# An attention and mixture-of-experts kernel: the last group's places scattered before the first expert's tokens are scaled, tokens transposed tile by tile, the first expert in two halves of 240 columns

## The chip, the cores and the metric

The kernel runs on one core of one Trainium2 chip. The metric is device time in microseconds (us), the median of several executions. A profile of one execution stands beside it; the prediction's sums are made against that execution.

## What is computed

Three stages are chained over 2304 tokens of 512 numbers (4 sequences of 576, 8 heads of 64).

```
scores = scale * q @ k.T                       # window of 32 keys: plain for heads 0-3, every 4th key for heads 4-7
x = softmax(where(mask, scores, -1e9)) @ v     # -> [2304, 512]

logits = x @ w_gate                            # 8 experts
e_idx = argmax(logits); gate_w = softmax(logits)[e_idx]; eom = sigmoid(x @ w_output_gate)
for e in range(8):                             # only tokens with e_idx == e
    out[mask] = gate_w * eom[:, e] * (relu(x[mask] @ w1[e]) @ w2[e])      # 512 -> 1024 -> 512

h = relu(out @ w_in); result = (h * h) @ w_out                            # 512 -> 2048 -> 512
```

## The kernel before

**Attention and routing.** Tokens come in 18 tiles of 128, in six groups (`GROUPS`: tiles 0-2, 3-6, 7-10, 11-12, 13-14, 15-17). For each tile TensorE multiplies q by k, VectorE and ScalarE make the softmax, TensorE multiplies by v, and the token rows x go to the table `x_d` in HBM (`store`, L495). For each group `lg` makes the gate's logits and `route1` to `route6` choose each token's expert and its place in that expert's list. `route5` (L580) ends with a cast of the places into the tile `di` (L599). `scatter` (L611, issue at L615) then has GpSimd write, by indirect DMA, one row per token into `meta_d`, the lists of all experts; a group of n columns takes n scatters. `di` comes from the pool `wk`, which has two buffers for each name, so a group's `di` has the buffer of the group two before it, and the cast waits until that group's scatters have landed.

**The first expert.** After group 4 (tokens 0 to 1919, `EARLY` = 15 tiles) `choose` picks the expert with most tokens so far. Its first weights are loaded (`load_w`, L114: pieces of 128 x 1024 numbers, 512 KB, eight to an expert, into three staging buffers `raw`), and the front of its list is read (`meta_load`, L133), its token rows gathered (`gather`, L138) and scaled (`scale`, L149) by the gate's weight while group 5 is still being routed. So the first expert is worked in two halves, `WD` entries 0 and 1, of `HALF` columns each: the first half holds only places that the first 1920 tokens have filled. `conv_w` (L119) splits a weight piece for the matmuls: ScalarE casts it to a reduced-precision float (L123), VectorE subtracts to get the rest (L124). `xsplit` (L154) does the same for tokens, ScalarE at L157 and VectorE at L158. Every product is three matmuls: high x high, high x low, low x high (`mm3`, L784).

**The order around the change** is written out by hand at the end of `attention` (L716 to L734): after the last tile come the logits of group 5, `warm(6)` (matmuls of ones that nobody reads), the conversion of weight piece 0, `route1` to `route4` of group 5, two more `warm` matmuls, the loads of pieces 2 and 3, the stores of the last tiles, then `scale(0)`, `transposes(0)` (L161), `conv_w(0, 1)`, `route5(5)`, and `scatter(5)`. `transposes(0)` takes both tiles of 128 tokens in turn, with the four blocks of 128 features of a tile going to four PSUM tiles in four banks; after the second tile it calls `xsplit` on each of the four.

**The experts** (`experts`, L736). GpSimd's queue starts with `meta_load(1)` and `gather(1)`, the second half of the first expert (L971, L972); the list of the second half needs the scatters of group 5. Then for each of the nine windows of `WD` come eight steps of `up` (L789: 12 matmuls, then ScalarE's relu L799 and VectorE's rest L800) and four of `down` (L805: 24 matmuls). In window 0, the first half, pieces 2 to 7 of the expert's weights are converted after steps 1, 3, 5, 6, 7 and 8. `scale(1)` stands after the second `down`, and `transposes(1)` after the third, so that the fourth `down` is behind them on TensorE. A window of n columns is 192 matmuls of n columns. The windows (`WIN`) are 512 (two halves of 256), 384, 336, 320, 304, 288, 256 and 256 columns for the experts in order of their size.

**The last stage** works on 2304 columns in six blocks of 384, and ends with indirect DMAs of the rows to their places.

Of the kernel before, what the change touches and what calls it, by code (L numbers as in the profile page):

```python
# [10 lines left out]
F32 = mybir.dt.float32  # L11
F32R = mybir.dt.float32r
BF16 = mybir.dt.bfloat16
I32 = mybir.dt.int32
# [9 lines left out]
P = 128  # L24
# [8 lines left out]
EARLY = GROUPS[NG - 1][0]  # L33
E = 8
# [1 line left out]
FF = 1024  # L36
FF2 = 2048

WIN = [512, 384, 336, 320, 304, 288, 256, 256]
HALF = WIN[0] // 2  # L40
MS = NT + 256
YC = sum(WIN) + 128
NEG = -8.0e9
# [9 lines left out]
def attention_experts_kernel(ctx: ExitStack, tc: tile.TileContext, qB, kB, vB, wg, wE, wF, consts, rows, ids, out):  # L53
    nc = tc.nc
# [11 lines left out]
    ident = cpool.tile([P, P], F32, name="ident")  # L66
# [35 lines left out]
    io32 = rowc[:, 4 * E + E * E:4 * E + E * E + NSPILL]  # L102


    WD = [(0, 0, HALF), (0, HALF, HALF)] + [(r, 0, WIN[r]) for r in range(1, E)]
    NW = len(WD)
    reg = {}

# [10 lines left out]
    def conv_w(r, c):  # L119
        s = free.pop(0)  # L120
        w_t[r, c] = s
        raw, (hi, lo) = raw_t.pop((r, c)), (slots[s][:, 0], slots[s][:, 1])
        nc.scalar.copy(out=hi, in_=raw)  # L123
        nc.vector.tensor_tensor(out=lo, in0=raw, in1=hi.bitcast(F32), op=ALU.subtract)  # L124


    xg_t, xh_t, xl_t = {}, {}, {}

    def tiles(w):
        n = WD[w][2]  # L130
        return [(i, min(P, n - P * i)) for i in range((n + P - 1) // P)]

    def meta_load(w, engine=None, n="p"):  # L133
        r, s0, _ = WD[w]
        k = len(tiles(w))
        (engine or nc.gpsimd).dma_start(out=mt[:, w, 0:k], in_=meta_d[ds(reg[n, r] * MS + s0, P * k), :].rearrange("(i p) c -> p i c", p=P))
# [9 lines left out]
            )  # L146
            xg_t[w, i] = t

    def scale(w):  # L149
        for i, n in tiles(w):  # L150
            t = xg_t[w, i]
            nc.vector.tensor_scalar(out=t[:n], in0=t[:n], scalar1=mt[:n, w, i, 1:2].bitcast(F32), scalar2=None, op0=ALU.mult)

    def xsplit(src, n):  # L154
        h = stg.tile([P, TB], F32R, tag="xh", name="xh", bufs=4)
        l = stg.tile([P, TB], F32R, tag="xl", name="xl", bufs=4)
        nc.scalar.copy(out=h[:, :n], in_=src)  # L157
        nc.vector.tensor_tensor(out=l[:, :n], in0=src, in1=h[:, :n].bitcast(F32), op=ALU.subtract)  # L158
        return h, l

    def transposes(w, bank, ks=range(4)):  # L161
        n = WD[w][2]
        p = {}
        for k, (i, m) in [(k, t) for k in ks for t in tiles(w)] if w else [(k, t) for t in tiles(w) for k in ks]:
            if i == 0:
                p[k] = bank(k)
            nc.tensor.transpose(p[k][:, P * i:P * i + m], xg_t[w, i][:m, P * k:P * k + P], ident[:m, :m])
            if w and i == len(tiles(w)) - 1:
                xh_t[w, k], xl_t[w, k] = xsplit(p[k][:, :n], n)
        if not w:  # L170
            for k in ks:
                xh_t[w, k], xl_t[w, k] = xsplit(p[k][:, :n], n)


    def row_pool(tp):
# [19 lines left out]
    def order_steps(tp):  # L195
# [4 lines left out]
        def row(shape, name, dt=F32):  # L200
            return tp.tile([1] + shape, dt, name=name)
# [40 lines left out]
        yield v.reduce_sum(out=low, in_=f16, axis=AX.X)  # L242
        yield v.tensor_scalar(out=low, in0=low, scalar1=float(HALF), scalar2=None, op0=ALU.is_lt)
        big = row([1], "big1")
        yield v.tensor_scalar(out=big, in0=of[:, E - 1:E], scalar1=float(NT - WIN[-1]), scalar2=low, op0=ALU.is_lt, op1=ALU.max)
        yield v.tensor_tensor(out=sr[:, 0, :], in0=win, in1=nw, op=ALU.subtract)
# [64 lines left out]
    def attention():  # L311
        st = ExitStack()
        c2 = st.enter_context(tc.tile_pool(name="c2", bufs=1))
        wk = st.enter_context(tc.tile_pool(name="wk", bufs=2))
        ps_s = st.enter_context(tc.tile_pool(name="ps_s", bufs=2, space=PSUM))
        ps_1 = st.enter_context(tc.tile_pool(name="ps_1", bufs=1, space=PSUM))
# [7 lines left out]
        def warm(n):  # L324

            ps = ps_1.tile([P, 4, P], F32, tag="xt", name="warm")
            for _ in range(n):
                nc.tensor.matmul(out=ps, lhsT=ones, rhs=ones.unsqueeze(1).to_broadcast([P, 4, P]), start=True, stop=True)
# [36 lines left out]
        o = 2 * P  # L365
# [129 lines left out]
        def store(i, m, engine=nc.sync):  # L495
            a = i % 2
            x = x_t["pair", i // 2]
            d = x_d[P * i:P * i + m * P]
            engine.dma_start(out=d[:, 0:256].rearrange("(n p) c -> p n c", n=m), in_=x[:, a:a + m, 0:256])
            for n in range(m):  # L500
                engine.dma_start(out=d[P * n:P * n + P, 256:512].rearrange("(j r) c -> r j c", r=4), in_=x[:, a + n, 256:512])
# [25 lines left out]
        def t3(g, name, dt=F32):  # L527
            return wk.tile([P, 4, E], dt, tag=name, name=name)[:, 0:COLS[g]]

        def t2(g, name, dt=F32):  # L530
            return wk.tile([P, 4], dt, tag=name, name=name)[:, 0:COLS[g]]
# [4 lines left out]
        def rows_of(g):  # L536
            return slice(0, 96 if len(GROUPS[g]) == 3 else P)
# [42 lines left out]
        def route5(g):  # L580

            ls, e, oh = rt[g]
            rk = rk_t.pop(g)
            n, c = rows_of(g), COLS[g]
            m = idsb[:, g, 0:c]
            v = nc.vector
            zp, z, ez, se, dn = t3(g, "zp"), t2(g, "z"), t2(g, "ez"), t2(g, "se"), t2(g, "dn")
            r1, s2, di = t3(g, "r1"), t2(g, "s2"), t2(g, "di", I32)
            v.tensor_tensor(out=zp[n], in0=oh[n], in1=ls[n, :, E:2 * E], op=ALU.mult)
            v.reduce_sum(out=se[n], in_=e[n], axis=AX.X)  # L590
            v.reduce_sum(out=z[n], in_=zp[n], axis=AX.X)
            nc.scalar.activation(out=ez[n], in_=z[n], func=ACTF.Exp, scale=-1.0)
            v.tensor_tensor(out=r1[n], in0=rk[n, 0:c], in1=eoff[n, 0:c], op=ALU.add)
            v.tensor_scalar(out=se[n], in0=se[n], scalar1=1e-9, scalar2=None, op0=ALU.add)
            v.tensor_tensor(out=r1[n], in0=r1[n], in1=oh[n], op=ALU.mult)
            v.scalar_tensor_tensor(out=dn[n], in0=ez[n], scalar=1.0, in1=se[n], op0=ALU.add, op1=ALU.mult)
            v.reduce_sum(out=s2[n], in_=r1[n], axis=AX.X)
            v.reciprocal(out=m[n, :, 1:2].bitcast(F32), in_=dn[n].unsqueeze(2))
            v.tensor_copy(di[n], s2[n])  # L599
            rt[g] = di, m, oh  # L600
# [10 lines left out]
        def scatter(g, cols=None):  # L611
            di, m, _ = rt[g]
            n = rows_of(g)
            for b in cols or range(COLS[g]):
                ins = nc.gpsimd.indirect_dma_start(  # L615
                    out=meta_d, out_offset=bass.IndirectOffsetOnAxis(ap=di[n, b:b + 1].bitcast(U32), axis=0),
                    in_=m[n, b, :], in_offset=None, bounds_check=E * MS - 1, oob_is_err=False,
                ).ins
                for o in scat:
                    tc.declare_no_dep(ins, o, reason="each slot of a list is written once")  # L620
                scat.append(ins)
# [14 lines left out]
        for i in range(EARLY):  # L636
# [3 lines left out]
            t = (i + 2) % LAP  # L640
            n = i + 2 - t + LAP
# [21 lines left out]
            g = ends.get(i - 1)  # L663
# [16 lines left out]
        i, g = EARLY, NG - 2  # L680
# [44 lines left out]
        load_w(0, 3)  # L725
        store(i + 1, 1)
        store(i + 2, 1)
        scale(0)
        transposes(0, lambda k: ps_1.tile([P, 1024 if k == 2 else 512], F32, tag=("pt", "lg", "o", "xt")[k], name="xT"))
        conv_w(0, 1)  # L730
        route5(g + 1)
        scatter(g + 1)
        nc.vector.tensor_copy(cs[:, 1, :], cnt[0:1, :])
        return st  # L734

    def experts():  # L736
# [22 lines left out]
        def placed():  # L759
            v = loaded(of_t, ACTE, sum(WIN) - WIN[-1], "sums of at most the windows' lengths")  # L760
            oa.update(enumerate(v))
# [27 lines left out]
        def up(w, f):  # L789
            r, _, n = WD[w]  # L790
            s = slots[w_t[r, f // 2]]
# [13 lines left out]
        def down(w, c):  # L805
            r, _, n = WD[w]
            s = w_t[r, 4 + c]
# [6 lines left out]
            nc.scalar.copy(out=y[:, :n], in_=p[:, :n])  # L814
            at = slice(HALF * w, HALF * w + n) if w < 2 else ds(oa[r], n)
            nc.scalar.dma_start(out=yT_d[P * c:P * c + P, at], in_=y[:, :n])
# [3 lines left out]
        def ids_out(w):  # L820
            r, s0, n = WD[w]
            at = slice(HALF * w, HALF * w + n) if w < 2 else ds(oa[r], n)
            nc.scalar.dma_start(out=idc_d[at, :], in_=meta_d[ds(reg["a", r] * MS + s0, n), :])
# [326 lines left out]
def _consts():  # L1150
# [20 lines left out]
    lt = (e[None, :] < e[:, None]).astype(f)  # L1171
    rows = np.concatenate([e, E - 1 - e, np.array(WIN, f), e * MS, lt.reshape(-1), np.arange(NSPILL, dtype=f)])[None]
    return dict(consts=consts, rows=np.ascontiguousarray(rows), ids=np.ascontiguousarray(ids.reshape(P, -1)))
# [14 lines left out]
```

## Time and profile before

| what | us |
|---|---|
| median of 3 runs | 793.91 |
| lowest, highest | 791.36, 796.9 |
| the profiled execution, its own time | 794.1 |
| its span, first to last instruction | 792.4 |
| TensorE busy in the span | 736.1 (93%) |
| VectorE, ScalarE, GpSimd busy | 437.1, 328.7, 94.6 |

PE is TensorE's matmuls, PEld its weight loads, DVE VectorE, ACT ScalarE, POOL GpSimd, SP the engine that issues most DMAs. A row of a timeline gives start, duration, engine, line, operation, the tiles (written, then read), the number of instructions merged in the row, and in square brackets the time for which the engine had stood idle and what ended that. A matmul's duration is longer than the step to the next one, since matmuls overlap; a rate is read from the starts.

### The profile page before, as it was taken

The numbers are of one execution on the slowest core, as the hardware profiler recorded it, in microseconds if no ns is written. First come the engines' busy times: TensorE is split into PE (matmuls) and PEld (weight loads), VectorE is DVE, ScalarE is ACT, GpSimd is POOL, SyncE is SP. The second block draws the span as 40 slices with busy tenths as digits, with TensorE's granted clock in tenths as the row PEclk, the third lists the DMA queues.
The fourth block names the chain that finished last, engine by engine and source line by source line (L and its number), as shares of the span: only waits on it lengthen the run. The fifth ranks groups of instructions, "written<-read, shape, count | busy, mean of one in ns | idle before, by whom it ended". The sixth has DMA issues, their size and how long they took to land. (4 is left out here: it accounts for less than half of the span.)

```text
span 792.4 us, 13859 instructions
## 1 busy us (share of the span) xinstructions
PE 736.1 (93%) x5363; PEld 670.6 (85%) x5363; DVE 437.1 (55%) x888; ACT 328.7 (41%) x647; POOL 94.6 (12%) x104
## 2 busy tenths in 40 slices
PE   8767759899999999999999999999999999999993
PEld 5555539899999999999999989999889888889992
DVE  7656636477566566777677787762333333332421
ACT  3433324364454555655555555552222222222320
POOL 5234414320110110000000000000100000010101
PEclk9999869899999999999999999999999999999997
DMA  8999457474666667765444334330302012030201
GB/s 275 296 274 255 119 171 191 137 244 142 223 185 200 201 200 218 213 216 166 129 159 134 124 116 160 107 119 1 97 23 91 29 45 76 10 111 1 81 1 43
DMA packets 55073, 110.54 MB, mean 140 GB/s; under 512 B 9497, under 2 KB 30874, under 8 KB 55002
## 3 DMA queue, kind: packets, MB, share of 16 engines
q1 hardware_dynamic: 45338, 93.35, 39.0%
q0 software_dynamic: 4192, 10.77, 3.8%
q10 hardware_dynamic: 5472, 5.48, 2.0%
q8 instruction: 44, 0.72, 0.4%
q14 instruction: 27, 0.22, 0.1%
HBM read 89.62 MB, written 20.00 MB: 138 GB/s over the span
## 5 line engine op out<-in xcount | busy, mean ns | idle before, releaser
L785 PE MATMUL hp<-xh,slot 128*128 128x384 f32 (+5 forms) x672 | 216.4, 322 | 1.2 <-DVE hl L800 1.2
L787 PE MATMUL hp<-xh,slot 128*128 128x384 f32 (+5 forms) x672 | 216.1, 322 | 0.0
L786 PE MATMUL hp<-xl,slot 128*128 128x384 f32 (+5 forms) x672 | 215.7, 321 | 0.0
L785 PEld LDWEIGHTS hp<-xh,slot 128*128 128x128 f32 x672 | 127.7, 190 | 4.8 <-DVE hl L800 1.4
L786 PEld LDWEIGHTS hp<-xl,slot 128*128 128x128 f32 x672 | 127.7, 190 | 3.2 <-DVE xl L158 0.2
L787 PEld LDWEIGHTS hp<-xh,slot 128*128 128x128 f32 x672 | 127.6, 190 | 0.0
L872 DVE SCALAR_TENSOR_TENSOR g<-hp,r 128x384 f32<-128x384 f32 x96 | 53.2, 554 | 120.3 <-ACT r L871 119.8
L899 PE MATMUL op<-slot,gh 128*128 128x512 f32 x288 | 112.5, 390 | 1.9 <-ACT gh L874 1.9
L901 PE MATMUL op<-slot,gl 128*128 128x512 f32 x288 | 113.9, 395 | 0.0
L900 PE MATMUL op<-slot,gh 128*128 128x512 f32 x288 | 113.3, 393 | 0.0
L124 DVE TENSOR_TENSOR slot<-raw,slot 128x1024 fp32r<-128x1024 f32 x64 | 77.8, 1224 | 52.3 <-ACT slot L123 52.2
L871 ACT ACTIVATE r<-hp 128x384 f32<-128x384 f32 x96 | 46.9, 489 | 142.1 <-PE hp L787 141.7
L786 PE MATMUL yp<-hl,slot 128*128 128x256 f32 (+5 forms) x288 | 87.0, 302 | 1.3 <-DVE hl L800 1.2
L785 PE MATMUL yp<-hh,slot 128*128 128x256 f32 (+5 forms) x288 | 88.1, 306 | 0.1
L787 PE MATMUL yp<-hh,slot 128*128 128x256 f32 (+5 forms) x288 | 86.6, 301 | 0.0
L876 DVE TENSOR_TENSOR gl<-g,gh 128x384 fp32r<-128x384 f32 x96 | 53.5, 557 | 44.0 <-ACT gh L874 43.4
L874 ACT CAST gh<-g 128x384 fp32r<-128x384 f32 x96 | 49.2, 513 | 62.9 <-DVE g L872 62.5
L913 POOL DMA_INDIRECT out<-os,idc x18 | 17.6, 976 | 469.3 <-DVE os L912 467.8
L123 ACT CAST slot<-raw 128x1024 fp32r<-128x1024 f32 x64 | 66.4, 1051 | 14.0 <-DMA raw<-in_wE 9.4
L901 PEld LDWEIGHTS op<-slot,gl 128*128 128x128 f32 x288 | 54.0, 188 | 12.5 <-DVE gl L876 1.2
L899 PEld LDWEIGHTS op<-slot,gh 128*128 128x128 f32 x288 | 54.1, 188 | 12.3 <-ACT gh L874 3.2
L900 PEld LDWEIGHTS op<-slot,gh 128*128 128x128 f32 x288 | 54.0, 188 | 9.7
(152 smaller groups left out, 879.8 us busy)
## 6 DMA issues: line engine op xcount, KB each, us to landing
raw<-in_wE SPq DMA_DIRECT2D x63, 512.0 KB, 4.0
raw<-in_wF SPq DMA_DIRECT2D x32, 512.0 KB, 3.7
yr<-yT_d SPq DMA_DIRECT2D x48, 192.0 KB, 3.3
vb<-in_vB SPq DMA_DIRECT2D x16, 520.0 KB, 8.4
part_d<-os SPq DMA_DIRECT2D x18, 256.0 KB, 2.0
raw<-part_d SPq DMA_DIRECT2D x18, 256.0 KB, 4.3
q<-in_qB SPq DMA_DIRECT2D x8, 512.0 KB
x_d<-x SPq DMA_DIRECT2D x22, 128.0 KB
```

The lines of the kernel that those rows point to most:

```text
L123: nc.scalar.copy(out=hi, in_=raw)
L124: nc.vector.tensor_tensor(out=lo, in0=raw, in1=hi.bitcast(F32), op=ALU.subtract)
L785: nc.tensor.matmul(out=out, lhsT=wh, rhs=mh, start=first, stop=False)
L786: nc.tensor.matmul(out=out, lhsT=wh, rhs=ml, start=False, stop=False)
L787: nc.tensor.matmul(out=out, lhsT=wl, rhs=mh, start=False, stop=last)
L871: nc.scalar.activation(out=r, in_=p[:, :TB], func=ACTF.Relu)
L872: nc.vector.scalar_tensor_tensor(out=q, in0=p[:, :TB], scalar=0.0, in1=r, op0=ALU.max, op1=ALU.mult)
L874: nc.scalar.copy(out=h, in_=q)
L876: nc.vector.tensor_tensor(out=l, in0=q, in1=h.bitcast(F32), op=ALU.subtract)
L899: nc.tensor.matmul(out=o_t[j], lhsT=h[:, a], rhs=w[:, 0], start=first, stop=False)
L900: nc.tensor.matmul(out=o_t[j], lhsT=h[:, a], rhs=w[:, 1], start=False, stop=False)
L901: nc.tensor.matmul(out=o_t[j], lhsT=l[:, a], rhs=w[:, 0], start=False, stop=last)
```

## The change

Five edits. The window of the first expert is 480 columns instead of 512, and `HALF` is 240 (15 x 128 / 8), so 32 fewer columns are worked. `di` gets a tag of its own with four buffers. `conv_w(0, 1)`, `route5`, `scatter` of group 5 and the copy of the counts now stand ahead of the scaling of the first half's tokens. Three more `warm` matmuls follow them. The first half's tokens are then scaled and transposed tile by tile, with five `warm` matmuls between the two tiles; the four feature blocks go to two PSUM banks of the pool `ps_s`, two blocks of 256 columns in each, instead of to four banks. (`scale` can now take one tile alone, and `transposes` has lost its branch for window 0; for the other windows both do what they did.)

```
-WIN = [512, 384, 336, 320, 304, 288, 256, 256]
-HALF = WIN[0] // 2
+WIN = [480, 384, 336, 320, 304, 288, 256, 256]
+HALF = EARLY * P // E
...
-            r1, s2, di = t3(g, "r1"), t2(g, "s2"), t2(g, "di", I32)
+            r1, s2, di = t3(g, "r1"), t2(g, "s2"), wk.tile([P, 4], I32, tag="di", name="di", bufs=4)[:, 0:c]
...
         store(i + 2, 1)
-        scale(0)
-        transposes(0, lambda k: ps_1.tile([P, 1024 if k == 2 else 512], F32, tag=("pt", "lg", "o", "xt")[k], name="xT"))
         conv_w(0, 1)
+
         route5(g + 1)
         scatter(g + 1)
         nc.vector.tensor_copy(cs[:, 1, :], cnt[0:1, :])
+        warm(3)
+        banks = [ps_s.tile([P, 512], F32, tag="s", name="xT") for _ in range(2)]
+        for t in tiles(0):
+            scale(0, t)
+            j, n = t
+            for k in range(4):
+                nc.tensor.transpose(banks[k // 2][:, 256 * (k % 2) + P * j:256 * (k % 2) + P * j + n], xg_t[0, j][:n, P * k:P * k + P], ident[:n, :n])
+            if j == 0:
+                warm(5)
+        n = WD[0][2]
+        for k in range(4):
+            xh_t[0, k], xl_t[0, k] = xsplit(banks[k // 2][:, 256 * (k % 2):256 * (k % 2) + n], n)
```

On VectorE, at the end of the routing of group 5 and the start of window 0, these instructions stood in a row before (`xg` are gathered tokens, `xl` the low part of the transposed ones, `slot` a converted weight piece, `di` the places):

```order
L565 TENSOR_TENSOR oh<-eq,m_1779 96x32
L152 TENSOR_SCALAR xg<-xg,mt 128x512 x2
L158 TENSOR_TENSOR xl<-xT,xh 128x256 x4
L124 TENSOR_TENSOR slot_91<-raw,slot_91 128x1024
L589 TENSOR_TENSOR zp<-oh,ls 96x32
L590 TENSOR_REDUCE se<-ex 96x4
L591 TENSOR_REDUCE z<-zp 96x4
```

and now, at the end of `route5` of group 5, which has its line 592 to 595 here, this stands in a row:

```order
L592 SCALAR_TENSOR_TENSOR dn<-ez,se 96x4
L593 TENSOR_REDUCE s_1810<-r_1809 96x4
L594 RECIPROCAL idsb<-dn 96x4
L595 CAST di<-s_1810 96x4
L728 COPY cs<-rk 1x8
L153 TENSOR_SCALAR xg<-xg,mt 128x512
L153 TENSOR_SCALAR xg<-xg,mt 112x512
L159 TENSOR_TENSOR xl<-xT,xh 128x240 x4
L807 SCALAR_TENSOR_TENSOR hl<-hp,hh 128x240 x2
```

The weight piece, the ten instructions of `route5` and the copy of the counts have moved from behind the tokens' scaling and splitting to ahead of them.

On ScalarE, at the same place, before (with what each instruction waits for; `xh` is the high part of the transposed tokens):

```order
L552 ACTIVATE ex<-d 96x32 [waits DVE_49]
L157 CAST xh<-xT 128x256 [waits PE_49] x4
L123 CAST slot_91<-raw 128x1024 [waits DMAHW7_49]
L592 ACTIVATE ez<-z 96x4 [waits DVE_49]
L799 ACTIVATE hh<-hp 128x256 [waits DMAHW4_49,DMAHW6_49,DMAHW1_49,PE_49]
```

and now:

```order
L548 ACTIVATE ex<-d 96x32 [waits DVE_49]
L124 CAST slot_91<-raw 128x1024 [waits DMAHW7_49]
L588 ACTIVATE ez<-z 96x4 [waits DVE_49]
L158 CAST xh<-xT 128x240 [waits PE_49]
L158 CAST xh<-xT 128x240 [waits DVE_49]
L158 CAST xh<-xT 128x240 [waits PE_49]
L158 CAST xh<-xT 128x240 [waits DVE_49]
L806 ACTIVATE hh<-hp 128x240 [waits DMAHW4_49,DMAHW6_49,DMAHW1_49,PE_49]
```

The second and the fourth cast, which share a bank with the one ahead of them, now wait for VectorE, which reads that bank too.

## Rows read from the trace of the kernel before

**Rows 1.** Windows by stage: length; busy us of PE, PEld, DVE, ACT, POOL; clock; DMA.
```profile
115.00:148.41 33.41, 29.23 (x202) 28.46 (x202) 19.58 (x55) 13.28 (x26) 16.49 (x18) 0.82 0.60 160
148.41:171.46 23.05, 23.05 (x196) 23.05 (x195) 17.07 (x36) 13.47 (x26) 3.64 (x3) 1.00 0.52 161
171.46:782.20 610.74, 603.71 (x3437) 560.49 (x3435) 332.86 (x582) 263.07 (x504) 30.42 (x31) 1.00 0.38 121
```

**Rows 2.** Windows cut where TensorE's granted clock changes; columns as in rows 1.
```profile
106.43:120.08 13.65, 8.27 (x37) 6.57 (x37) 5.31 (x21) 2.67 (x7) 2.38 (x3) 0.50 0.55 164
120.08:140.56 20.48, 18.18 (x149) 17.67 (x147) 12.59 (x28) 9.54 (x16) 10.00 (x12) 1.00 0.76 204
140.56:147.39 6.83, 4.95 (x24) 4.87 (x24) 2.91 (x10) 1.49 (x4) 4.74 (x6) 0.50 0.40 112
```

**Rows 3.** Timeline, DVE: the end of route5 of group 4.
```profile
92.57 0.17 DVE L598 RECIPROCAL idsb<-dn 128x2 f32<-128x2 f32 x1
94.25 0.17 DVE L599 CAST di<-s 128x2 int32<-128x2 f32 x1 [1.51 <-DMA meta_d<-idsb,di]
```

**Rows 4.** Timeline: from the scatters of group 4 to the first half's tokens.
```profile
94.70 0.99 POOL L615 DMA_INDIRECT meta_d<-idsb,di  x1 [2.45 <-DVE rs L479]
...
105.13 1.05 POOL L142 DMA_INDIRECT xg<-x_d,mt  x1 [8.16 <-DMA x_d<-x]
...
110.06 0.49 DVE L152 TENSOR_SCALAR xg<-xg,mt 128x512 f32<-128x512 f32 x1 [3.35 <-DMA xg<-x_d,mt]
...
113.53 0.48 DVE L152 TENSOR_SCALAR xg<-xg,mt 128x512 f32<-128x512 f32 x1 [2.98 <-DMA xg<-x_d,mt]
```

**Rows 5.** Timeline: the first half's second tile, its split, and matmuls of window 0.
```profile
114.07 1.11 PE L167 MATMUL xT<-ident,xg 128*128 128x128 f32 x4 [2.35 <-DVE xg L152]
114.58 1.20 ACT L157 CAST xh<-xT 128x256 fp32r<-128x256 f32 x4 [8.42 <-PE xT L167]
114.98 1.42 DVE L158 TENSOR_TENSOR xl<-xT,xh 128x256 fp32r<-128x256 f32 x4 [0.97 <-ACT xh L157]
...
116.05 0.41 PE L785 MATMUL hp<-xh,slot 128*128 128x256 f32 x1
...
119.68 0.41 PE L787 MATMUL hp<-xh,slot 128*128 128x256 f32 x1
```

**Rows 6.** Timeline: from the scatters of group 5 to the second half's tokens on TensorE.
```profile
119.32 1.01 POOL L615 DMA_INDIRECT meta_d<-idsb,di  x1 [11.21 <-DVE cs L733]
...
129.38 0.76 POOL L136 DMA_DIRECT2D mt<-meta_d  x1 [5.36 <-DMA meta_d<-idsb,di]
...
134.03 1.07 POOL L142 DMA_INDIRECT xg<-x_d,mt  x1 [3.90 <-DMA mt<-meta_d]
...
140.31 0.33 PE L167 MATMUL xp<-ident,xg 128*128 128x128 f32 x1 [2.13 <-DVE xg L152]
...
141.98 0.49 DVE L152 TENSOR_SCALAR xg<-xg,mt 128x512 f32<-128x512 f32 x1 [1.72 <-DMA xg<-x_d,mt]
...
142.52 1.75 PE L167 MATMUL xp<-ident,xg 128*128 128x128 f32 x7 [1.88 <-DVE xg L152]
143.93 0.56 PE L785 MATMUL yp<-hh,slot 128*128 128x256 f32 x1
```

**Rows 7.** Timeline, PE: starts of matmuls of 256 and of 384 columns at full clock.
```profile
148.41 0.28 PE L785 MATMUL hp<-xh,slot 128*128 128x256 f32 x1
...
151.17 0.28 PE L787 MATMUL hp<-xh,slot 128*128 128x256 f32 x1
...
179.51 0.33 PE L785 MATMUL hp<-xh,slot 128*128 128x384 f32 x1
...
182.45 0.33 PE L787 MATMUL hp<-xh,slot 128*128 128x384 f32 x1
```

**Rows 8.** Timeline, ACT: weight pieces 5 and 6 of window 0 being cast.
```profile
128.93 1.05 ACT L123 CAST slot<-raw 128x1024 fp32r<-128x1024 f32 x1 [0.82 <-DMA raw<-in_wE]
...
131.88 1.05 ACT L123 CAST slot<-raw 128x1024 fp32r<-128x1024 f32 x1 [1.62 <-DMA raw<-in_wE]
```

More of the change, by code (lines that the diff above doesn't have):

```diff
@@ L102, in attention_experts_kernel @@
     io32 = rowc[:, 4 * E + E * E:4 * E + E * E + NSPILL]
-    WD = [(0, 0, HALF), (0, HALF, HALF)] + [(r, 0, WIN[r]) for r in range(1, E)]
+    WD = [(0, 0, HALF), (0, HALF, WIN[0] - HALF)] + [(r, 0, WIN[r]) for r in range(1, E)]
     NW = len(WD)
@@ L147, in gather, with scale @@
             xg_t[w, i] = t
-    def scale(w):
-        for i, n in tiles(w):
+    def scale(w, only=None):
+        for i, n in tiles(w) if only is None else [only]:
             t = xg_t[w, i]
@@ L162, in transposes @@
         n = WD[w][2]
[L163 to L172, printed above, removed]
+        for k in ks:
+            p = bank(k)
+            for i, m in tiles(w):
+                nc.tensor.transpose(p[:, P * i:P * i + m], xg_t[w, i][:m, P * k:P * k + P], ident[:m, :m])
+            xh_t[w, k], xl_t[w, k] = xsplit(p[:, :n], n)
     def row_pool(tp):
```

## The prediction

> **What bounds the kernel now.** First the busy time of each engine by stage. From 171.46 us on TensorE is busy for 603.71 of 610.74 us, and from 148.41 to 171.46, in the second half of the first expert, for all of it, at full clock [rows 1]. There only fewer or shorter matmuls would help. From 115.00 to 148.41, in the first half of the same expert, it is busy for 29.23 of 33.41 us at a mean clock of 0.82 [rows 1]. The work is the same 192 matmuls and takes 10.36 us longer (33.41 - 23.05). So the stretch before 148.41 is the place to look at.
>
> Then the clock. TensorE was granted 0.50 (1.2 GHz) from 106.43 to 120.08 and again from 140.56 to 147.39, and 1.00 (2.4 GHz) between and after [rows 2]. In the first of the two it worked for 8.27 of 13.65 us, waits for tokens between [rows 2]; the second came right after it had stood idle for 2.13 us [rows 6].
>
> Then, by the timeline, what it waited for. The first expert needs tokens that are scaled at 110.06 and 113.53, after waits of 3.35 and 2.98 us for the gather; the gather itself was issued at 105.13, at the end of a chain that starts with the scatters of group 4 at 94.70 [rows 4]. The second half needs the scatters of group 5. GpSimd had stood idle for 11.21 us when it could issue the first of them at 119.32, because `route5` stood behind the first half's tokens on VectorE. From there the chain runs on: read of the list 129.38, gather 134.03, last tokens scaled 141.98 [rows 6], 22.7 us in all (141.98 - 119.32). TensorE waits for it, 2.13 and 1.88 us [rows 6].
>
> **The change part by part.**
>
> A. The places' own buffers. The cast of group 4's places waited 1.51 us for the scatters of group 2 [rows 3], and the scatter, `choose`, the list and the gather of rows 4 all hang on it. With four buffers group 4 has group 0's, whose scatters are long done. What is late next is data that is there: the products of the tile that follows it. I let the whole 1.5 us come through to the first tokens (bounds: 0, if the gather is held by other transfers, to 1.5).
>
> B. The clock at the start. Between 116.05 and 119.68 lie 17 matmul steps, 0.2135 us each; at full clock 23 steps take 2.76 us, 0.120 each [rows 5, 7]. So a step at half clock costs 0.0935 more. Some 20 matmuls from 115.00 to 120.08 run so: 1.9 us, and the four transposes of the second tile, 1.11 us merged [rows 5], lose another 0.4. The change lays five filler matmuls into the wait of 2.35 us before the second tile, and three before the first. If TensorE then has its full clock when the split is done, 2.3 us go. The fillers themselves run where it would wait. I take 2.0 (bounds 0 and 2.3).
>
> C. The split costs more. Before, four casts on ScalarE took 1.20 us and four subtractions on VectorE 1.42, shifted by 0.40 (114.58 and 114.98): 1.82 in all [rows 5]. Two blocks now share a bank, and the order has the second and fourth cast wait for VectorE. Then a cast (0.30), a subtraction (0.36), and so on alternate, with an overlap only where the bank changes: about 2.6 us. The first `up` also writes a bank that the split still reads. Loss 0.8 (bounds 0 and 1.5).
> The Trainium skill has a rule for this (PSUM — Partial Sum Buffer, Terms): no two of the three engines may access one bank in the same cycle, reads against reads included. In rows 5 the blocks had a bank each and the engines did overlap, which agrees; by the rule C is the 0.8 that I take, without it C would be 0 and the time 0.8 lower.
>
> D. The second half's list. `route5` and the weight piece ahead of the scaling fill the 3.35 us for which VectorE waited for the gather anyway [rows 4], so they delay nothing. The places are then ready near 108 instead of 119, and the scatters go out some 11 us earlier. With the same 22.7 us the second half's tokens are scaled near 131, and TensorE, which came to that place at 138.18 (140.31 - 2.13), comes to it near 135 after A to C and half of E, and need not wait. What goes: from the first transpose's wait to the next `down` it took 2.13 + (143.93 - 140.31) = 5.75 us, and eight transposes without a wait need about 1.0 at full clock (seven took 1.75 at half [rows 6]), so 4.75. Then sixteen matmuls between 143.93 and 147.39 at half clock, 16 x 0.0935 = 1.5 us. Together 6.2 (bounds 2 and 6.2). The second half's list read and gather stay on the same queue, and nothing else is moved past them.
>
> E. Fewer columns. Two windows of 192 matmuls lose 16 columns each. Steps of 0.120 us for 256 columns and 0.173 for 384 (17 steps from 179.51 to 182.45) [rows 7] give 0.42 ns per column, so 6.7 ns a matmul, and 384 x 6.7 ns = 2.6 us. But no matmul of this kind in the profile has fewer than 256 columns. Bounds: from 2.6 gained to what the third rival says. I take the straight line, which the rows keep between 256 and 384.
>
> F. What gets late next in window 0. The weights come through three buffers: pieces 5 and 6 were cast at 128.93 and 131.88 after waits of 0.82 and 1.62 us for their transfers [rows 8], each of which starts when an earlier piece is converted. Piece 4 now starts some 9 us earlier, since piece 1 is converted earlier; the others follow TensorE's own steps and shift with it, but TensorE's steps get shorter than the transfers. Also the scaling of the second half's tokens stands behind piece 7 on VectorE. I put 1.0 us on this (bounds 0 and 3).
>
> Sum: 1.5 + 2.0 - 0.8 + 6.2 + 2.6 - 1.0 = 10.5 us. The profiled execution took 794.1 us, span 792.4 and 1.7 around it, and stands 0.2 above the median of 793.91, so no correction is made: 794.1 - 10.5 = 783.6 us. That is 1.3% less. A measurement of this kernel tells about 1% from no change, 7.9 us.
>
> **The rivals.**
>
> 1. The narrow matmul takes as long as one of 256 columns. For it: none shorter is to be seen, and at each step a weight load of 128 columns goes by; against it: the line from 384 to 256 shows no bend [rows 7]. Then E is gone: 786.2.
>
> 2. The second half's tokens stay late, or a weight piece does. The chain of rows 6 is mostly transfer time, 5.36 and 3.90 us in two waits; now it runs beside the stores of the last tiles and two weight loads. If TensorE still waits 2 us and its clock drops once more, D shrinks to 2.5: 787.3. Against it: some 4 us of slack by D.
>
> 3. Slower: the matmul of 240 columns is slower than that of 256. Place: all 384 matmuls of windows 0 and 1. For the price the trace has a second kind of row: plain fp32 transposes of 128 columns, seven in 1.75 us at half clock [rows 6], step by step as long as a matmul of 256 columns there (0.21), so two cycles a column. If a matmul below 256 columns fell to that rate it would cost like 480 columns, 0.214 us: 384 x 0.094 = 36 us more, against gains of 7.9 in A to D and F: 822. It decides from 0.141 us a matmul (7.9 / 384 = 0.021 above 0.120). For it only that every window is 256 or more; against it that the type and the three products stay the same.
>
> 4. The clock stays low to 120 in spite of the fillers; B gives 0: 785.6. For it: after 115.00 the engine worked without a gap and still had its full clock only from 120.08 [rows 2]; against it: the fillers start the work some 3 us sooner.
>
> 5. What moves was hidden after all, by transfers that hold both gathers: about 791.
>
> **How the numbers follow.** Forecast 0.38, rival 1 0.20, rival 2 0.12, rival 3 0.15, rival 4 0.10, rival 5 0.05. Faster by over 1% means under 786.0: nearly all of the forecast (0.36), half of rivals 1 and 4 (0.15), a little of 2 (0.01): 0.52. Slower by over 1% is rival 3: 0.15. The rest, 0.33, lies within 1%. The range goes from all gains at their upper bounds with C and F at 0 (12.6, which is 781.5, and 1.5 for the spread of the runs) to rival 5: 780.0 to 791.0. It leaves out rival 3 and a few hundredths. The forecast's own range is 781.5 to 786.
>
> **What would show it.** The cast of group 4's places without a wait, and the first half's last tokens scaled near 112. Scatters of group 5 before 110. A granted clock of 1.00 at the first `up` and no drop until the end. No wait of TensorE for scaled tokens before the fourth `down` of window 0, which then ends near 139. Steps of 0.113 us in windows 0 and 1. I am wrong if the step is 0.120 or more (E), if TensorE waits for `xg` again (D), if weight casts wait longer than 2 us for their transfers (F), or if the clock is 0.50 after 115 (B).

## The result and the profile after

The changed kernel takes 784.93 us, the median of 6 runs (782.14 to 789.08); the kernel before, beside it, 792.95 us (791.36 to 796.9). The ratio is 0.9899, with a 95% interval from 0.9866 to 0.9932: 8.0 us, or 1.0%, less. The forecast was 783.6. The profiled execution took 785.35 us, with a span of 783.6, 8.8 less than the span before.

First the windows, which answer to [rows 1] and [rows 2]: busy time by stage, then cut where the granted clock changes (columns as there).
```profile
117.41:141.99 24.58, 24.25 (x201) 24.06 (x201) 15.19 (x39) 11.38 (x22) 11.55 (x14) 0.94 0.58 180
141.99:165.01 23.02, 23.02 (x206) 22.89 (x205) 17.31 (x40) 14.16 (x26) 4.79 (x4) 1.00 0.62 184
165.01:783.60 618.59, 602.37 (x3426) 559.30 (x3424) 332.70 (x582) 262.13 (x503) 30.51 (x30) 0.99 0.37 119
...
99.95:110.19 10.24, 6.50 (x81) 3.81 (x81) 4.61 (x13) 4.07 (x10) 2.69 (x3) 1.00 0.85 190
110.19:120.43 10.24, 7.23 (x28) 5.30 (x28) 3.82 (x18) 1.60 (x6) 4.08 (x5) 0.50 0.55 194
120.43:141.99 21.56, 21.24 (x189) 21.04 (x188) 14.52 (x37) 10.96 (x21) 11.46 (x14) 1.00 0.66 203
```
The first half of the first expert went from 33.41 to 24.58 us: TensorE now works through it with 0.33 us of idle time, and the second stretch at a clock of 0.50 [rows 2] is gone. But it starts 2.4 us later (117.41 against 115.00), and the first stretch at 0.50 still reaches into it, to 120.43. The second half went from 24.33 (148.41 to 172.74, the same 192 matmuls with the transposes between them) to 23.02, and what follows took 618.59 us against 619.66 (172.74 to the end).

Then the timeline after, whose rows answer to [rows 3] to [rows 7].
```profile
95.79 0.17 DVE L594 RECIPROCAL idsb<-dn 128x2 f32<-128x2 f32 x1
95.99 0.17 DVE L595 CAST di<-s 128x2 int32<-128x2 f32 x1
96.44 0.98 POOL L611 DMA_INDIRECT meta_d<-idsb,di  x1 [1.33 <-DVE rs L475]
...
111.54 0.47 DVE L153 TENSOR_SCALAR xg<-xg,mt 128x512 f32<-128x512 f32 x1
111.83 1.05 POOL L611 DMA_INDIRECT meta_d<-idsb,di  x1 [2.87 <-DVE cs L728]
...
113.00 0.49 DVE L153 TENSOR_SCALAR xg<-xg,mt 112x512 f32<-112x512 f32 x1 [0.99 <-DMA xg<-x_d,mt]
...
115.73 0.36 ACT L158 CAST xh<-xT 128x240 fp32r<-128x240 f32 x1 [4.78 <-issue]
116.12 0.41 DVE L159 TENSOR_TENSOR xl<-xT,xh 128x240 fp32r<-128x240 f32 x1 [2.63 <-ACT xh L158]
116.56 0.62 ACT L158 CAST xh<-xT 128x240 fp32r<-128x240 f32 x2 [0.47 <-issue]
116.95 0.72 DVE L159 TENSOR_TENSOR xl<-xT,xh 128x240 fp32r<-128x240 f32 x2 [0.42 <-ACT xh L158]
117.41 0.57 PE L792 MATMUL hp<-xh,slot 128*128 128x240 f32 x1 [1.35 <-DVE xl L159]
117.71 0.36 ACT L158 CAST xh<-xT 128x240 fp32r<-128x240 f32 x1 [0.53 <-DVE xl L159]
118.00 0.42 PE L794 MATMUL hp<-xh,slot 128*128 128x240 f32 x1
118.10 0.41 DVE L159 TENSOR_TENSOR xl<-xT,xh 128x240 fp32r<-128x240 f32 x1 [0.42 <-ACT xh L158]
...
119.92 0.41 PE L794 MATMUL hp<-xh,slot 128*128 128x240 f32 x1
...
120.34 0.76 POOL L137 DMA_DIRECT2D mt<-meta_d  x1 [3.60 <-DMA meta_d<-idsb,di]
123.17 1.05 POOL L143 DMA_INDIRECT xg<-x_d,mt  x1 [2.06 <-DMA mt<-meta_d]
...
136.71 0.88 DVE L153 TENSOR_SCALAR xg<-xg,mt 128x512 f32<-128x512 f32 x2
138.44 1.00 PE L167 MATMUL xp<-ident,xg 128*128 128x128 f32 x8
139.21 0.36 PE L792 MATMUL yp<-hh,slot 128*128 128x240 f32 x1
...
141.99 0.27 PE L792 MATMUL hp<-xh,slot 128*128 128x240 f32 x1
...
142.77 0.27 PE L793 MATMUL hp<-xl,slot 128*128 128x240 f32 x1
```
The cast of group 4's places has no wait. The scatters of group 5 start at 111.83 instead of 119.32, and the second half's tokens are scaled at 136.71, so TensorE comes to them at 138.44 without a wait, and all eight transposes take 0.77 us (138.44 to 139.21). The split of the first half, four casts and four subtractions, runs from 115.73 to 118.51, 2.78 us against 1.82 [rows 5], and the first `up` waits 1.35 us in the middle of it. A full-clock step of 240 columns is 0.111 us here (7 steps in 0.78) against 0.120 for 256 [rows 7]. At half clock it is 0.213 (9 steps from 118.00 to 119.92), the same as for 256 columns in [rows 5].

Last the row that answers to [rows 8], in the view of the waits of ScalarE from 100 to 165 us (total, times, longest).
```profile
ACT slot L124 <- DMA raw<-in_wE: 3.7, 5, 1.2
```
The casts still wait for weights, but TensorE has no wait for a piece in this stage.

### The profile page after: what moved, and what is told of

Its sections match the earlier page's. It is cut to its first block, busy times and chain, and to the rows that moved or that the text cites. A ratio compares the mean times of both kernels' runs of the same rounds, so it can differ in the third digit from the quotient of the medians.

```text
span 783.6 us, 13876 instructions
## 1 busy us (share of the span) xinstructions
PE 736.5 (94%) x5371; PEld 669.0 (85%) x5371; DVE 435.4 (56%) x888; ACT 327.8 (42%) x647; POOL 94.5 (12%) x104
## 5 line engine op out<-in xcount | busy, mean ns | idle before, releaser
L792 PE MATMUL hp<-xh,slot 128*128 128x384 f32 (+6 forms) x672 | 215.6, 321 | 2.5 <-DVE xl L159 1.3
L794 PE MATMUL hp<-xh,slot 128*128 128x384 f32 (+6 forms) x672 | 215.4, 320 | 0.0
L793 PE MATMUL hp<-xl,slot 128*128 128x384 f32 (+6 forms) x672 | 214.8, 320 | 0.0
L793 PE MATMUL yp<-hl,slot 128*128 128x240 f32 (+6 forms) x288 | 85.9, 298 | 1.4 <-DVE hl L807 1.3
L792 PE MATMUL yp<-hh,slot 128*128 128x240 f32 (+6 forms) x288 | 86.9, 302 | 0.1
L794 PE MATMUL yp<-hh,slot 128*128 128x240 f32 (+6 forms) x288 | 85.5, 297 | 0.0
```

Of the source, the lines that this page charges most:

```text
L792: nc.tensor.matmul(out=out, lhsT=wh, rhs=mh, start=first, stop=False)
L793: nc.tensor.matmul(out=out, lhsT=wh, rhs=ml, start=False, stop=False)
L794: nc.tensor.matmul(out=out, lhsT=wl, rhs=mh, start=False, stop=last)
```

## The experiments

The kernels ran in three sets, each with its own runs of the kernel before beside it, so ratios are compared across sets and times only within one; the first set also ran on another chip than the second and third. In the first set the kernel before took 794.51 us (median), in the second 796.41, in the third 798.3.

**The changed kernel again.** No edit.

> The changed kernel once more, unaltered, to stand beside the next three on the same chip. In its first profile the engines stood still from 86.4 to 90.5 us and the first `up` came at 117.41 us, 2.4 us later than in the kernel before. Theory: that pause is chance of one execution and no work of the change; then it is gone here, the first `up` starts between 112 and 115.5 us and the profiled execution takes 781 to 783.5 us. Rival: it follows from the change (the four buffers, or another order of transfers); then it stands here again at the same place and the first `up` starts near 117.4. The median ratio to the kernel before is 0.988 to 0.992 in either case.

Measured: 785.57 us, ratio 0.9905 (0.9885 to 0.9926). The pause is shorter, a wait of ScalarE of 2.6 us against 4.3; the first `up` starts at 114.72, and the span is 782.0. So the pause does not follow from the change, but it is no accident of one execution either: ScalarE waits so, for 2.6 to 4.8 us between 84 and 94 us, in 11 of the 14 profiles, the second one of the kernel before among them (4.3), and the profile doesn't tell for what. The first profile of the kernel before, from which all rows of the prediction were taken, is one of the three without it. Over all profiles the first `up` starts between 114.7 and 121.5, in the two of the kernel before at 115.0 and 117.5, so its start at 117.41 is no work of the change. The timeline shows something else:
```profile
109.67 0.49 DVE L153 TENSOR_SCALAR xg<-xg,mt 112x512 f32<-112x512 f32 x1 [0.35 <-DMA xg<-x_d,mt]
110.28 2.34 PE L324 MATMUL warm<-ones 128*128 128x512 bf16 x5
112.41 0.95 PE L735 MATMUL xT<-ident,xg 112*128 112x112 f32 x4
```
Here the second tile was scaled at 110.16, and its transposes waited for the five fillers until 112.41. In this execution the fillers did not lie in a wait, they were the wait.

**The windows of before in the new order.**
```diff
-WIN = [480, 384, 336, 320, 304, 288, 256, 256]
+WIN = [512, 384, 336, 320, 304, 288, 256, 256]
-HALF = EARLY * P // E
+HALF = WIN[0] // 2
```

> The changed order with the windows of before (512 columns, halves of 256): what the narrower half is worth. Theory (the columns count): a full-clock step goes from 0.112 back to 0.120 us, 0.007 to 0.008 us for about 370 steps, so 2.6 to 3.0 us slower than the changed kernel, a ratio to the kernel before of 0.992 to 0.995. Rival (the first two windows are bound by the weights' transfers, not by columns): same time as the changed kernel within 0.8 us, with longer waits for `raw` in the changed kernel's window 0.

Measured: 788.30 us, 2.7 more than the changed kernel in the same set, ratio 0.9932 (0.9913 to 0.9951). In the windows by stage both halves lose: the first takes 25.72 us against 24.72 in the repeat above, the second 24.34 against 22.82.
```profile
115.32:141.04 25.72, 25.72 (x200) 25.72 (x201) 16.01 (x41) 11.61 (x22) 12.38 (x14) 0.92 0.61 179
141.04:165.38 24.34, 24.34 (x207) 24.34 (x206) 17.20 (x37) 14.53 (x26) 4.09 (x4) 1.00 0.58 181
```
So the columns count, by about what the straight line had. The intervals of the two ratios overlap a little, but the traces don't: the second half takes 24.3 us in all four profiles with halves of 256 columns, and 22.8 to 23.0 in all ten with 240.

**The list put back behind the split.**
```diff
-        route5(g + 1)
-        scatter(g + 1)
-        nc.vector.tensor_copy(cs[:, 1, :], cnt[0:1, :])
         warm(3)
...
             xh_t[0, k], xl_t[0, k] = xsplit(...)
+        route5(g + 1)
+        scatter(g + 1)
+        nc.vector.tensor_copy(cs[:, 1, :], cnt[0:1, :])
```

> The changed kernel with `route5`, the scatters of the last group and the copy of the counts put back behind the first tokens' transposes and split; everything else stays. Theory (the early list is nearly the whole gain): TensorE waits for the second half's tokens again, 2 us or more in two waits, and drops to a granted clock of 0.50 after it; 4.5 to 6.5 us slower than the changed kernel, a ratio to the kernel before of 0.995 to 0.999. Rival 1 (only the wait counts, the clock does not drop again): 2 to 4 us slower. Rival 2 (the columns, fillers and buffers made the gain): within 1 us of the changed kernel.

Measured: 792.56 us, median of 12 runs (787.58 to 797.3), 7.0 more than the changed kernel (4.5 to 6.5 were expected), ratio 0.9980 (0.9965 to 0.9995). But the profiled execution was the lowest of the twelve, 787.58, and shows no lost time: the read of the list waited only 1.4 us for the scatters, and the tokens were scaled by 138.5, just as TensorE came to them (it waited 0.2 us). So one more profile was taken.

> A second profile of the kernel with the last group's list put back behind the first split. Its median was 7.0 us above the changed kernel's (792.56 against 785.57), but its first profile, the lowest of its 12 times, had no wait for the second half's tokens, because the read of the list waited only 1.4 us for the scatters, against 5.36 in the kernel before. Theory (a near miss: the tokens come at 138 and TensorE at 138): here the tokens are scaled after 140, TensorE waits for them 1 us or more, its granted clock falls to 0.50 again before 150, and the execution takes 790 to 794 us. Rival (the lost time lies elsewhere): the time is above 790 with no such wait and no second fall of the clock.

Measured: 796.53 us, above the expected 790 to 794 and level with the kernel before in its set. GpSimd and TensorE in its timeline, then the window at the lower clock:
```profile
131.50 0.76 POOL L137 DMA_DIRECT2D mt<-meta_d  x1 [5.12 <-DMA meta_d<-idsb,di]
136.59 1.05 POOL L143 DMA_INDIRECT xg<-x_d,mt  x1 [4.34 <-DMA mt<-meta_d]
...
142.26 0.33 PE L167 MATMUL xp<-ident,xg 128*128 128x128 f32 x1 [2.33 <-DVE xg L153]
145.08 1.65 PE L167 MATMUL xp<-ident,xg 112*128 112x112 f32 x7 [2.49 <-DVE xg L153]
146.40 0.55 PE L792 MATMUL yp<-hh,slot 128*128 128x240 f32 x1
```
```profile
142.47:149.29 6.82, 4.33 (x21) 4.22 (x21) 2.82 (x10) 1.44 (x4) 5.02 (x6) 0.50 0.44 110
```
Waits of 5.12 us for the scatters and 4.34 for the list, against 3.60 and 2.06 in the changed kernel; TensorE idle for 2.33 and 2.49 us; and the clock down for 6.82 us. That is the picture of [rows 6]. The mechanism is the one forecast. Its size in one execution hangs on how long the transfers take: this order has no slack, so with a wait of 1.4 us for the scatters window 0 took 26.08 us, and with one of 5.1 it took 32.20.

**The kernel before, a second profile.** No edit.

> The kernel before once more, unaltered, for a second profile. In its first one TensorE waited 2.13 and 1.88 us for the second half's tokens and its clock was 0.50 from 140.56 to 147.39. Theory (that is what the early list takes away in nearly every execution): a wait of TensorE for those tokens of 1.5 us or more is here too, and a second stretch at 0.50 after it. Rival (it was chance of that one profile): no such wait, and window 0 ends near 143 instead of 148.4.

Measured: 797.02 us. TensorE waited 2.23 and 2.81 us for the second half's tokens, the clock was 0.50 again from 145.10 to 148.51, and window 0 took 33.17 us (33.41 in the first profile). So that loss is not the first profile's alone. What is the first profile's alone is the wait of [rows 3]: here the cast follows with no wait, with the two buffers of before.
```profile
96.74 0.17 DVE L598 RECIPROCAL idsb<-dn 128x2 f32<-128x2 f32 x1
96.95 0.17 DVE L599 CAST di<-s 128x2 int32<-128x2 f32 x1
```

**The early list alone, on the kernel before.**
```diff
-        scale(0)
-        transposes(0, ...)
         conv_w(0, 1)
         route5(g + 1)
         scatter(g + 1)
         nc.vector.tensor_copy(cs[:, 1, :], cnt[0:1, :])
+        scale(0)
+        transposes(0, ...)
```

> The kernel before with one step of the change alone: `conv_w(0, 1)`, `route5`, the scatters of the last group and the copy of the counts go ahead of the first tokens' scaling; windows, transposes, fillers and buffers stay. Theory (the early list is most of the gain): 5 to 7 us faster, a ratio of 0.991 to 0.994, no wait of TensorE for the second half's tokens and no second fall of its clock. Rival 1 (the order only pays with the tile-by-tile transposes and the fillers): within 2 us of the kernel before. Rival 2 (`route5` and the weight piece delay the first tokens): the first `up` starts 1 to 2 us later and the gain is 3 to 5 us.

Measured: 789.84 us against 796.41, 6.6 less, ratio 0.9920 (0.9896 to 0.9945). Window 0 has 256 columns as before and no idle time at all:
```profile
119.60:144.71 25.11, 25.11 (x202) 24.94 (x201) 16.72 (x43) 12.01 (x24) 13.48 (x15) 0.96 0.66 194
```
This one change of order makes some four fifths of the gain.

**The narrow window alone, on the kernel before.**
```diff
-WIN = [512, 384, 336, 320, 304, 288, 256, 256]
+WIN = [480, 384, 336, 320, 304, 288, 256, 256]
```

> The kernel before with one step of the change alone: the first expert's window is 480 columns, in halves of 240. Theory (the columns count in the second half at full clock, and little where the clock is 0.50 or TensorE waits for tokens): 192 steps of window 1 by 0.008 us, 1.5 us, and at most 0.5 us of window 0, because the second half's tokens set its end: 1.3 to 2.0 us faster, a ratio of 0.9975 to 0.9985. Rival 1 (all 384 steps count): 2.6 to 3.1 us, 0.996 to 0.997. Rival 2 (the narrower window makes TensorE come earlier to a wait that stays): no faster, 0.999 or more.

Measured: 795.50 us against 796.41, ratio 0.9991 (0.9972 to 1.001). Not told apart from no change, nor from 1.5 us. In its profile the second half took 22.82 us (24.33 before), as the columns have it; in the first half TensorE still waited for tokens. The first set gives 2.7 us for the same step once the list is early; here, with the tokens late, the medians differ by 0.9.

**The fillers.**
```diff
-        warm(3)
...
-            if j == 0:
-                warm(5)
```

> The changed kernel without the eight fillers in front of and between the first transposes. Theory (they bring nothing): the granted clock still rises at about 120.4 us, the same share of the first `up` runs at half clock, and the time is that of the changed kernel within 0.8 us. Rival 1 (they bring the rise forward): without them the clock is 0.50 some 5 to 10 us longer after the first `up`, 24 to 48 steps of 0.2135 instead of 0.112 us, so 2.4 to 4.9 us slower. Rival 2 (they are in the way): the transposes of the second tile come 0.5 to 1.5 us earlier and the time is lower by as much.

Measured: 787.15 us against 785.57 for the changed kernel, but the ratios are 0.9899 (0.9877 to 0.9920) and 0.9905 (0.9885 to 0.9926): not told apart. The window at 0.50 in its profile:
```profile
109.23:122.88 13.65, 7.86 (x35) 6.66 (x33) 5.30 (x19) 1.91 (x6) 5.60 (x7) 0.50 0.54 180
```
It reaches 5.3 us past the first `up` at 117.60, against 3.0 us in the first profile of the changed kernel (117.41 to 120.43) and 4.0 in the second. But without fillers there it reached 5.1 and 3.7 us past it in the two profiles of the kernel before, and 2.2 us with the early list alone. It is therefore not shown that the fillers bring the rise forward; the table in the next section sets their price beside it.

**Two buffers for the places.**
```diff
-            r1, s2, di = t3(g, "r1"), t2(g, "s2"), wk.tile([P, 4], I32, tag="di", name="di", bufs=4)[:, 0:c]
+            r1, s2, di = t3(g, "r1"), t2(g, "s2"), t2(g, "di", I32)
```

> The changed kernel with `di` back in its two buffers. Theory (the wait is hidden: in the unaltered repeat of the changed kernel the first `up` came only 0.28 us before that of the kernel before, so four buffers gave next to nothing): within 0.8 us of the changed kernel, a ratio to the kernel before of 0.989 to 0.992, though the cast of group 4's places waits again for a scatter, by up to 1.5 us. Rival (the step of 1.5 us comes through as forecast): 1.2 to 1.8 us slower, 0.992 to 0.9935, with the first gather and the first `up` that much later.

Measured: ratio 0.9895 (0.9860 to 0.9929), that of the changed kernel. In its profile the cast did not wait:
```profile
98.27 0.17 DVE L594 RECIPROCAL idsb<-dn 128x2 f32<-128x2 f32 x1
98.47 0.17 DVE L595 CAST di<-s 128x2 int32<-128x2 f32 x1
```
In five profiles of kernels with two buffers, the wait stands in one, the first. So this run does not measure what such a wait would cost.

**Four banks for the first transposes.**
```diff
-        banks = [ps_s.tile([P, 512], F32, tag="s", name="xT") for _ in range(2)]
+        banks = [ps_1.tile([P, 1024 if k == 2 else 512], F32, tag=("pt", "lg", "o", "xt")[k], name="xT") for k in range(4)]
```
(The transposes and the split then take `banks[k]`; the fillers write a tile of `ps_s`.)

> The changed kernel with a PSUM bank for each of the four blocks of first transposes, as in the kernel before; the eight fillers write another bank then. Theory (two blocks in a bank make ScalarE and VectorE take turns): the first to the last instruction of the split take 1.8 us instead of 2.8, the first `up` no longer waits 1.35 us behind the first subtraction, and the kernel is 1.0 to 1.5 us faster than the changed one, a ratio of 0.987 to 0.990. Rival (the sharing costs nothing, the alternation has another cause): the split takes 2.6 us or more here too.

Measured: 786.17 us, ratio 0.9866 (0.9825 to 0.9908). The split in its timeline:
```profile
116.92 1.15 ACT L158 CAST xh<-xT 128x240 fp32r<-128x240 f32 x4 [6.23 <-issue]
117.31 1.35 DVE L159 TENSOR_TENSOR xl<-xT,xh 128x240 fp32r<-128x240 f32 x4 [2.02 <-ACT xh L158]
117.33 0.57 PE L792 MATMUL hp<-xh,slot 128*128 128x240 f32 x1
```
1.74 us (116.92 to 118.66) instead of 2.78, both engines at work beside each other, and the first `up` starts 0.41 us into it, without a wait. The Trainium skill (PSUM — Partial Sum Buffer, Terms) lets no two of these engines into one bank in the same cycle. The alternation does go with the shared bank, but as a wait for VectorE (0.53 us before the last cast in the changed kernel); what the bank would do without that wait no run here shows.

**A version meant to beat both.**
```diff
-        warm(6)
+        warm(18)
...
-        warm(2)
+        warm(8)
...
-        warm(3)
...
-            if j == 0:
-                warm(5)
```
(With four banks as above.)

> A version meant to beat both: four banks as in the run beside it, the eight fillers ahead of and between the first transposes taken out, and 18 more laid where TensorE waits some 4 us for the last group's route (18 instead of 6 there, 8 instead of 2 behind it). Theory (TensorE's clock falls for that wait, and between the transposes the fillers stand in the way of tokens that are there): the granted clock is 1.00 at the first `up` and stays so, the first `up` comes 1 to 3 us earlier relative to the second scaling, and the kernel is 2 to 4 us faster than the changed one, a ratio of 0.985 to 0.988. Rival 1 (the clock falls in spite of them, as it did in the changed kernel): only the 1 us of the banks and up to 2 us of the fillers, 0.987 to 0.990. Rival 2 (more fillers delay the route of the last group): as slow as the changed kernel or slower.

Measured: 786.44 us, ratio 0.9869 (0.9828 to 0.9909): as the four banks alone, which is the first rival. The clock held through the route's wait and fell later, for the waits of 2.34 and 1.80 us for the tokens:
```profile
114.56:121.39 6.83, 5.80 (x26) 5.41 (x27) 2.44 (x6) 1.52 (x5) 2.39 (x3) 0.50 0.31 108
```
By the ratios both of these versions would be some 3 us faster than the changed kernel, but the intervals overlap, so that is not shown.

**Columns below 240.**
```diff
-WIN = [480, 384, 336, 320, 304, 288, 256, 256]
+WIN = [480, 384, 336, 320, 304, 288, 208, 192]
-YC = sum(WIN) + 128
+YC = sum(WIN) + 240
```

> The changed kernel with the last two windows at 208 and 192 columns instead of 256 (the tokens that these two experts have fit in them; the outputs stay whole). It measures the price of a column below 240 at full clock. Theory (straight line): steps of 0.099 and 0.092 us, so 192 x (0.021 + 0.028) = 9.4 us faster than the changed kernel, a ratio of 0.977 to 0.981. Rival 1 (a floor near 0.112 us, set by the weight load that goes with each step): 2 to 3.5 us faster, steps of 0.11 in both. Rival 2 (the straight line for TensorE, but the experts' weights cannot come faster than 20 to 22 us each): TensorE waits in the last two windows and 4 to 6 us are gained.

Measured: 788.31 us, ratio 0.9875 (0.9829 to 0.9921), so no 9 us, but the first rival. TensorE's starts in the two windows, 14 steps of 208 columns and 21 of 192:
```profile
339.83 0.27 PE L792 MATMUL yp<-hh,slot 128*128 128x208 f32 x1
...
341.39 0.28 PE L794 MATMUL yp<-hh,slot 128*128 128x208 f32 x1
...
362.63 0.27 PE L794 MATMUL yp<-hh,slot 128*128 128x192 f32 x1
...
364.97 0.28 PE L794 MATMUL yp<-hh,slot 128*128 128x192 f32 x1
```
1.56 / 14 and 2.34 / 21 are both 0.111 us, the step of 240 columns. There is a floor, and 240 columns lie on it.

## Why the prediction came out right

Times read from the profiles: from the start of the second tile's scaling to the first `up`, from there to the first `down` (96 matmuls), and the length of window 0.

| kernel | scaled to `up` | `up` to `down` | window 0 |
|---|---|---|---|
| before, first and second profile | 1.48, 1.48 | 13.96, 13.38 | 33.41, 33.17 |
| changed, first and second profile | 4.41, 5.05 | 12.36, 12.79 | 24.58, 24.72 |
| changed, last windows narrow | 4.06 | 12.73 | 25.26 |
| changed, two buffers for the places | 2.72 | 12.55 | 25.32 |
| without the fillers | 2.90 | 13.42 | 25.26 |
| four banks | 2.53 | 11.54 | 23.61 |
| meant to beat both | 1.64 | 13.37 | 25.20 |
| early list alone | 1.48 | 12.72 | 25.11 |

**A, forecast 1.5, measured about 0.** The step that failed is "I let the whole 1.5 us come through". The wait of [rows 3] was read from one execution; it is not there in four other profiles with two buffers. The first profile is also the one of the five without the pause of ScalarE. In it the places of group 4 were ready soon after the last scatter of group 2, whose buffer they take, was issued (timeline of the kernel before, GpSimd):
```profile
86.78 0.98 POOL L615 DMA_INDIRECT meta_d<-idsb,di  x1 [0.31 <-issue]
```
They were ready 6.0 us after that (92.57 + 0.17, [rows 3]) and the buffer was free 7.5 us after it, at 94.25. In every other profile 8.0 us or more passed between the two, so by an estimate from this one landing none of them would have waited. What the wait costs in an execution that has it, no run shows. Moreover the cast itself comes at 93.2 to 95.3 us in the first set and at 96.1 to 99.2 in the second and third, a larger spread than the term.

**B, forecast 2.0, measured near 0.** The step "the fillers themselves run where it would wait" failed. At half clock the five take 2.34 us, and when the tokens are on time they hold them: 4.41 and 5.05 us from scaling to `up` with the fillers, 2.90 without. Where the second tile came late, as in the run with two buffers (scaled from 117.28, the first from 114.46), the same fillers did lie in the wait, and it took 2.72. They give back 0.6 to 1.1 us up to the first `down`. The clock was not full at the first `up` in either profile of the changed kernel (in the run with two buffers it was 1.00 from 117.23 on, and 0.50 again from 120.64 to 124.06). A clock below full there is rival 4, and its 785.6 is nearer to the median than the forecast.

**C, forecast -0.8, measured -1.4.** The mechanism stood: the split lasts 2.78 us. The price was undersized. The sum took a quarter of a merged row of overlapping instructions for each, 0.30 and 0.36, where a cast alone takes 0.36 and a subtraction 0.41. And what counts is not the end of the split but the second subtraction, the last to read the first bank: the first `up` starts at 117.41, right behind it (116.95 + 0.41), where with a bank each it starts at 117.33, next to the first one (117.31). That is 2.90 - 1.48 = 1.4 us without fillers, and with four banks and no fillers it is back at 1.64.

**D, forecast 6.2, measured 6.6 and 7.0** (the early list alone, and taken back). Right in mechanism, and a little over its upper bound, by less than the noise of the medians. From the first wait to the next `down` eight transposes take 0.77 us without a wait, not the 1.0 put down, and the waits can be longer than in the first profile (5.0 us together in the second profile of before, against 4.0). The clock's second fall is gone, as forecast, and rivals 2 and 5 fell. The places on the time axis were too early in the first profile (scatters at 111.83 instead of before 110, the end of the fourth `down` at 141.99 instead of near 139) and right in the second (109.14 and 139.44).

**E, forecast 2.6, measured 2.7.** Rivals 1 and 3 fell: the step is shorter, not equal and not longer. (The rows give 0.41 ns a column, not 0.42, which makes 2.5.) That the sum came out rests on the line being read where it ends: 16 columns further down it would have given 0.107 us, below the 0.111 at which the step stops. The step at half clock, 0.213 us for either size, was not foreseen; it concerns the first 14 to 19 steps (3.0 to 4.0 us).

**F, forecast -1.0, measured 0 to -0.9.** The casts waited for transfers (3.7 us in one profile; 7.7 in the other, the longest 2.5, over the 2 us that the prediction named as a sign), but they did so before the change too (4.2 and 5.1 in its two profiles, the longest 1.8 and 2.5). TensorE was held only through VectorE's remainders of the hidden values, 0.3 us in the first profile, nothing in the second, 0.9 in that with two buffers, against 0.2 and 0.4 before the change. So a loss by F is not told from none.

Sum: 7.0 + 2.7 - 1.4 - 0.3 = 8.0, with A and B at 0. Measured 8.0 and, in the first set, 8.9. That it comes out to the tenth is luck: by their intervals the differences behind D and E are known to some 2 us each. The forecast of 10.5 was too high by A and B, 3.5 us, and got 1.0 of that back in C to F taken together. So the time fell close to the forecast because the two terms that carried it, D and E, were right; the two that were read as gains at the start of window 0 were not there. And a part of the closeness is luck: the kernel before took 792.95 us beside the changed one, not the 794.1 that the sum started from, which hid 1.15 of the 2.5 us by which the gain was forecast too high.

## What to carry to other kernels

Move the producer of a late list ahead of work that only waits anyway, and judge it by its slack against the slowest transfers, not the typical ones: the late order lost next to nothing in its fastest execution and 7 us in the median. A wait of 1.5 us that hangs on a transfer needs a second profile before it is counted as a gain. Fillers stand in front of the work behind them: data that was on time waited 2.25 us behind five of them (110.16 to 112.41 in the repeat). And at the lower clock they are about twice as long, 2.34 us there against 1.24 at full clock in the second profile of the late order.

## What was not expected of the hardware

The step of these matmuls with 128-column weights stops falling at 0.111 us at full clock: 240, 208 and 192 columns all take it, while 256 take 0.120 and 384 take 0.173. At half clock 240 and 256 columns both take 0.213. The Trainium skill (TensorE: Matmul & The Clock Gate, LDWEIGHTS (loading the stationary operand)) gives a weight load in ns as its columns over 1.2. For 128 columns that is an estimate of 107 ns, and the floor lies near it. The profile's rows of these loads last 0.19 us each at full clock and overlap one another, so none shows that price. That the load is the floor's cause is argued, not shown, since no run here changed the weights' width.

The wait for the same four scatters to land, with nothing changed in the program, was 1.4 us in one execution of the late order and 5.1 in another, on another chip.
